# The first stage of a fused attention and SwiGLU kernel in another order

## The chip, the cores and the metric

The kernel runs on one core of one Trainium2 chip. The metric is the device time of one execution in microseconds (us). One execution was also recorded by the hardware profiler; times inside it are counted from the start of its span.

The engines are TensorE (PE, matrix products), VectorE (DVE), ScalarE (ACT), GpSimd (POOL) and SyncE (SP). Each works through its own instructions in order, and they meet by semaphores. Transfers (DMAs) are issued by SP, ACT and POOL; POOL's go through a queue of their own, the software queue.

## What is computed

Four batches, eight heads, 768 tokens, head size 64. Each token attends to the 96 tokens up to itself and to the first 8 of its batch (the global ones), with a bias that falls with the distance; then a feed-forward block over 3072 tokens.

```python
scores = scale * np.matmul(q, k.transpose(0, 1, 3, 2))
is_global = pos[None, :] < int(n_global)
is_local = (rel >= 0) & (rel < int(n_local))
keep = is_global | is_local
scores = np.where(keep, scores + bias, -1000000000.0)
a = softmax(scores)
x = (a @ v).transpose(0, 2, 1, 3).reshape(B * S, H * D)
g = x @ w_gate
out = g * sigmoid(g) * (x @ w_val) @ w_out
```

(512 columns to 1536 and back to 512.)

## The kernel before

**The order is written out.** A long string, ORDER, lists steps such as `T.1.0.0` or `x.0.1.0`. A table maps the name before the first point to a function, and the rest are its arguments. The steps are run one after the other under a manual schedule, so each engine does its instructions in the order in which the steps name them. An engine that waits holds up all that stands behind it on the same engine.

**Tiling.** Keys are cut in seven chunks of 120; to each chunk the 8 global keys are added, so that a chunk has 128 rows. A chunk's scores are for the 216 queries that can see it. Heads go in pairs (hp 0 to 3). Batch 0, the first to be worked on, is cut in two halves of 384 tokens, and each half's scores in two parts (u), one 432 wide per head (864 for the pair) and one 144 (288). A tile of the feed-forward block is half a batch (360 or 408 tokens).

**The steps of the first stage.**
- `fill` (L345): matmuls of constants, whose result is not used; each is 256 columns wide.
- `Lf` (L256) loads one head pair of the first half of keys or queries in float32 by SP or ACT; `cast` (L349) turns it into float16 on DVE or ACT. `Lh` (L260) loads other heads through POOL, where the transfer itself casts.
- `T` (L366): six transposes on PE, of one head pair and half of keys or queries. `k` (L379, L385) copies the transposed keys from PSUM into chunks on DVE or ACT and then spreads the eight global columns over all chunks on DVE. `q` (L395) copies the queries.
- `B` (L461): products of a slope times the identity (`sl`, L331) with the distances (L248, L253), which put the bias into the score bank. `c` (L474): the score products. `x` (L484): the exponential on ACT. `M` (L337) makes masks on ACT from the distances, and `m` (L502) multiplies by them; units with a bias need none.
- `w` (L537): denominator and numerators; `i` (L554, L555), `r` (L563), `p` (L574): the reciprocal of the denominator, its spread and the product that gives xT. `g`, `v` (L587): gate and value products, `t`, `s`, `h` (L594, L599, L609): the activation. `o` (L622): the output products; `e` (L632, L634): eviction on ACT and transfer on SP.
- `Lv` (L264) loads one chunk of the values, rows 8 and up. The rows 0 to 8 of chunks 1 to 6 hold the batch's first eight values. `LG` (L269) loads these for all four batches into a small tile vG; `G` (L277 by SP, L279 by an engine) copies them from there into the chunks. For chunk 0 the first rows are cleared.
- `D` (L432): transposes of later batches' keys and queries by DMA, issued on SP.

**PSUM.** Two double banks, S0 and S1, are taken in turn by scores and numerators; four single ones go to all others. So each second pair of score steps waits until the exponential of the one before last has been done.

**Around the change.** In ORDER, batch 0's first steps are: LG, the clearing and 16 fills; queries cast and transposed; keys cast on DVE, transposed and copied on DVE; then biases `B.1.1 B.1.0`, scores, and exponentials `x.0.1.0 x.0.1.1`, where the first unit sits in S1 and the second in S0; then the transposes of three more head pairs and `B.0.0`, which takes S0. Batch 0's global rows are copied by POOL in two halves (`G.0.1.4.P`, `G.0.4.7.P`), those of the others by SP (`G.1.0.7.S`, `G.2.0.7.S`, `G.3.0.7.S`). At the end, the last 128 tokens' output is made in two halves of 256 columns (`o.3.5.x.0` and `.1`), each with its eviction and transfer.

Of the kernel before, what the change touches and what calls it, by code (L numbers as in the profile page):

```python
# [10 lines left out]
FP16 = mybir.dt.float16  # L11
# [4 lines left out]
KC = 120  # L16
# [21 lines left out]
LG Li Z.0.P pre fill.14 sl.2 fill.2 Lf.A.1.0 cast.1.0.V sl.6 Ld.S T.0.0.1 q.0.0.V sl.3 Lf.A.1.1 dd  # L38
cast.1.1.A sl.1 T.1.0.1 Lf.S.0.1 cast.0.1.V Lh.0.0.4.8 T.1.0.0 k.1.0.V sl.0 Lf.S.0.0 cast.0.0.V
B.1.1 B.1.0 q.1.0.A c.0.1.0 M.5.0 c.0.1.1 M.1.1 T.0.0.0 k.0.0.V T.3.0.0 sl.4 k.3.0.V M.0.1 x.0.1.0  # L40
x.0.1.1 Lh.1.0.4.8 T.2.0.0 M.6.1 k.2.0.A M.7.1 B.0.0 c.0.0.0 x.0.0.0 B.0.1 c.0.0.1 x.0.0.1 T.2.0.1
T.3.0.1 q.3.0.V Lh.1.1.0.4 Lh.0.1.0.4 sl.5 T.1.1.0 Lh.1.1.4.8 q.2.0.V T.1.1.1 q.1.1.A Lv.0.1 k.1.1.V
T.0.1.1 c.0.3.1 Lv.0.2 Lv.0.0 B.2.0 Lh.0.1.4.8 Lw.0.0.0 x.0.3.1 c.0.2.0 q.0.1.V Lw.1.0.0 T.0.1.0
w.0.0.0.0 Lw.0.0.1 x.0.2.0 T.2.1.1 T.3.1.1 B.2.1 c.0.2.1 q.2.1.A sl.7 B.3.0 x.0.2.1 q.3.1.A
G.0.1.4.P c.0.3.0 x.0.3.0 Lw.1.0.1 M.3.0 w.0.0.0.1 i.0.0.0 Lw.0.1.0 m.0.3.1.P r.0.0.0 w.0.0.0.2
p.0.0.0.V T.3.1.0 T.2.1.0 w.0.1.0.0 i.0.1.0 B.1.2 c.0.1.2 r.0.1.0 w.0.1.0.1 k.3.1.A Lw.0.1.1
w.0.1.0.2 x.0.1.2 Lw.1.1.0 ga.0.0 Lw.1.1.1 ga.0.1 B.1.3 c.0.1.3 k.0.1.A p.0.1.0.V x.0.1.3 k.2.1.V
c.0.3.2 x.0.3.2 m.0.3.2.V g.0.3 gb.0.0 t.0.0 s.0.0 B.0.3 t.0.3 s.0.3 gb.0.1 t.0.1 Lw.0.2.1 c.0.0.2
c.0.0.3 x.0.0.3 s.0.1 v.0.3 h.0.3 v.0.0 x.0.0.2 v.0.1 Lw.0.2.0 h.0.1 g.0.4 g.0.7 L4.1.0 t.0.4 h.0.0
s.0.4 t.0.7 s.0.7 g.0.6 t.0.6 L4.0.0 M.4.1 s.0.6 ga.0.2 gb.0.2 t.0.2 M.3.1 v.0.4 Lv.0.5 h.0.4 v.0.6  # L50
c.0.2.3 s.0.2 m.0.0.2.P c.0.2.2 x.0.2.3 h.0.6 x.0.2.2 w.0.0.1.0 i.0.0.1 r.0.0.1 g.0.5 t.0.5
G.0.4.7.P s.0.5 v.0.2 v.0.7 M.2.1 h.0.7 g.0.8 h.0.2 g.0.9 M.5.1 t.0.8 s.0.8 v.0.5 Lv.0.3 M.6.0
g.0.11 Lv.0.4 t.0.9 s.0.9 h.0.5 Lv.0.6 Lw.1.2.0 t.0.11 s.0.11 g.0.10 t.0.10 c.0.3.3 s.0.10 m.0.2.3.V
m.0.2.2.P U.1.0 x.0.3.3 m.0.3.3.V U.0.1 U.1.1 kw.1.A U.0.0 qw.1.A w.0.0.1.1 w.0.0.1.2 p.0.0.1.V
w.0.1.1.1 w.0.1.1.0 Lw.1.2.1 Lr.1.0.6 w.0.1.1.2 i.0.1.1 c.1.1.1 Lr.1.0.7 v.0.9 r.0.1.1 p.0.1.1.V
kw.0.A Lr.1.1.7 qw.0.A v.0.8 x.1.1.1 h.0.8 h.0.9 M.7.0 v.0.10 Lr.1.0.4 g.1.6 Lr.1.1.4 c.1.0.0 t.1.6
x.1.0.0 c.1.0.1 D.1.3.0 v.0.11 h.0.11 h.0.10 g.1.0 t.1.0 s.1.0 x.1.0.1 c.1.1.0 g.1.9 t.1.9 g.1.7
s.1.6 t.1.7 s.1.9 g.1.1 s.1.7 x.1.1.0 g.1.3 v.1.0 t.1.3 Lr.1.0.5 h.1.0 v.1.6 D.1.2.0 c.1.0.2 s.1.3
h.1.6 c.1.1.2 K.1.3.A t.1.1 K.1.2.V g.1.5 s.1.1 x.1.1.2 M.2.0 M.0.0 v.1.9 h.1.9 v.1.7 t.1.5 h.1.7
Lr.1.1.6 Lr.1.1.5 D.1.3.1 s.1.5 g.1.2 t.1.2 x.1.0.2 s.1.2 D.1.2.1 v.1.5 g.1.11 t.1.11 h.1.5  # L60
m.1.0.1.P Lo.1 s.1.11 Lr.3.0.5 g.1.4 Lo.0 m.1.1.2.P v.1.3 h.1.3 t.1.4 m.1.0.2.V Lo.2 g.1.8 t.1.8
v.1.1 h.1.1 s.1.4 c.1.2.1 x.1.2.1 c.1.3.1 s.1.8 v.1.8 v.1.11 h.1.11 v.1.2 Lr.2.0.3 x.1.3.1 h.1.2
Lv.1.1 c.1.2.2 x.1.2.2 c.1.3.0 v.1.4 Lr.2.0.0 h.1.4 o.0.1.0 Z.1.V m.1.1.0.P M.4.0 Lr.2.0.2 m.1.3.1.V
G.1.0.7.S g.1.10 Lv.1.2 o.0.1.1 o.0.1.2 x.1.3.0 c.1.2.0 x.1.2.0 h.1.8 c.1.3.2 x.1.3.2 o.0.1.3 e.0.1
Lr.2.1.1 M.1.0 v.1.10 o.0.0.0 o.0.0.1 Lv.1.0 m.1.2.1.V m.1.1.1.V Lr.2.0.1 t.1.10 m.1.3.0.V o.0.0.2
o.0.0.3 o.0.2.0 o.0.2.1 m.1.2.2.V Z.2.V Lv.1.3 s.1.10 m.1.0.0.V w.1.0.1.0 e.0.0 w.1.0.0.1 w.1.0.0.0
h.1.10 m.1.2.0.P w.1.1.0.0 Lv.1.5 w.1.1.0.1 D.2.1.0 w.1.1.0.2 w.1.0.0.2 i.1.0.0 i.1.1.0 Lr.2.1.0
o.0.3.0 o.0.3.1 Lr.3.1.2 r.1.0.0 p.1.0.0.D D.2.0.0 o.0.3.2 o.0.3.3 Lv.1.6 r.1.1.0 Lv.1.4 Lr.2.1.4
p.1.1.0.D o.0.2.2 e.0.3 o.0.2.3 e.0.2 g.2.1 i.1.0.1 r.1.0.1 t.2.1 s.2.1 Lr.2.1.3 Lr.2.1.7 g.2.7
t.2.7 s.2.7 g.2.3 t.2.3 v.2.7 h.2.7 g.2.0 v.2.3 K.2.1.V Lr.3.0.1 g.2.5 s.2.3 K.2.0.V t.2.0 w.1.0.1.1  # L70
m.1.3.2.P w.1.1.1.1 w.1.1.1.0 D.2.0.1 s.2.0 w.1.1.1.2 Lr.2.1.2 D.2.1.1 i.1.1.1 w.1.0.1.2 o.0.4.0
t.2.5 s.2.5 Lr.2.0.7 Lr.2.0.6 o.0.4.1 o.0.4.2 o.0.4.3 p.1.0.1.D v.2.0 h.2.3 e.0.4 Lr.3.1.4 h.2.0
n.1.1.1 g.2.4 t.2.4 r.1.1.1 p.1.1.1.P D.2.3.0 v.2.1 h.2.1 s.2.4 g.2.11 t.2.11 s.2.11 g.2.2 t.2.2
# [27 lines left out]
G.3.0.7.S Lv.3.0 m.3.3.0.P v.5.10 h.5.0 g.5.1 t.5.1 o.2.1.0 h.5.10 w.3.1.0.0 s.5.1 i.3.1.0 w.3.1.0.1  # L101
# [15 lines left out]
o.3.5.3.0 o.3.5.0.1 o.3.5.1.1 o.3.4.1 o.3.4.2 e.3.5.0 o.3.4.3 e.3.4 o.3.5.2.1 o.3.5.3.1 e.3.5.1  # L117
"""
# [3 lines left out]
def kernel(  # L122
# [73 lines left out]
    vG = sb.tile([NG, B, H, D], FP16, name="vG")  # L196
# [47 lines left out]
    def ld_ident():  # L244
        nc.sync.dma_start(out=ident, in_=ident_dr.ap())
# [9 lines left out]
    def ld_first(e, i, hp):  # L255
        (nc.sync if e == "S" else nc.scalar).dma_start(  # L256
            out=h32[i][:, 2 * hp:2 * hp + 2, :], in_=tokens3(i, 0, 2 * hp, 2 * hp + 2))
# [10 lines left out]
    def ld_globals():  # L268
        nc.gpsimd.dma_start(  # L269
            out=vG.rearrange("p b h d -> p (b h) d"),  # L270
            in_=v[:, :, 0:NG, :].rearrange("b h p d -> p (b h) d"))

    def put_globals(b, c0, c1, e):
        src = vG[:, b, :, :].unsqueeze(1).broadcast_to([NG, c1 - c0, H, D])
        dst = v_of(b)[0:NG, c0:c1, :, :]
        if e == "S":
            nc.sync.dma_start(out=dst, in_=src)  # L277
        else:
            copy_on(e)(out=dst, in_=src)  # L279
# [68 lines left out]
    def cast(i, hp, e):  # L348
        copy_on(e)(out=h16[i][:, 0, 2 * hp:2 * hp + 2], in_=h32[i][:, 2 * hp:2 * hp + 2])  # L349
# [263 lines left out]
    def columns(side):  # L613
        return slice(0, DM) if side is None else slice(DM // 2 * side, DM // 2 * (side + 1))
# [73 lines left out]
```

## Time and profile before

| what | value |
|---|---|
| time, three runs | 241.26, 241.51, 241.61 us; median 241.51 |
| the profiled execution | 241.57 us |
| its span | 239.7 us (1.87 us lie around it) |
| busy PE, DVE, ACT, POOL | 97%, 66%, 49%, 53% of the span |
| mean clock granted to PE | 0.993 |
| DMA | 25.5 MB in 88,715 packets |

How to read it. A line of the timeline gives the start and the length of a run of like instructions in us, engine and line, operation, what is written and read, shape and number; in brackets stands how long the engine was idle before it and what ended the wait. Two instructions of one line may overlap on PE, which is pipelined, so their lengths don't add up. In a row of windows, the busy time of each engine in that stretch is followed by the granted clock of PE (1.00 is full) and by the DMA share, the mean busy share of the 16 DMA engines (it can exceed 1, since packets of several queues overlap).

### The profile page before, as it was taken

The numbers are of one execution on the slowest core, as the hardware profiler recorded it, in microseconds if no ns is written. First come the engines' busy times: TensorE is split into PE (matmuls) and PEld (weight loads), VectorE is DVE, ScalarE is ACT, GpSimd is POOL, SyncE is SP. The second block draws the span as 40 slices with busy tenths as digits, with TensorE's granted clock in tenths as the row PEclk, the third lists the DMA queues.
The fourth block names the chain that finished last, engine by engine and source line by source line (L and its number), as shares of the span: only waits on it lengthen the run. The fifth ranks groups of instructions, "written<-read, shape, count | busy, mean of one in ns | idle before, by whom it ended". The sixth has DMA issues, their size and how long they took to land.

```text
span 239.7 us, 5641 instructions
## 1 busy us (share of the span) xinstructions
PE 232.2 (97%) x2274; PEld 133.0 (55%) x2274; DVE 158.7 (66%) x351; ACT 117.8 (49%) x225; POOL 128.2 (53%) x136
## 2 busy tenths in 40 slices
PE   7799999999999999999999999999999999999994
PEld 4355666555455655555555555556566555565452
DVE  4587888687768785577876844687877843577000
ACT  3778777876505355666464446652142323232121
POOL 8996888599899098999974004699100000000000
PEclk9799999999999999999999999999999999999999
DMA  7999999999999999996999025323020110200042
GB/s 169 181 191 205 204 165 155 152 143 187 161 140 153 167 146 143 156 100 120 123 166 100 3 88 92 68 16 23 0 90 3 44 40 8 83 4 0 0 175 90
DMA packets 88715, 25.50 MB, mean 106 GB/s; under 512 B 78537, under 2 KB 85745, under 8 KB 88689
## 3 DMA queue, kind: packets, MB, share of 16 engines
q0 software_dynamic: 67520, 13.81, 68.8%
q1 hardware_dynamic: 20624, 10.94, 20.8%
q8 instruction: 18, 0.29, 0.5%
q10 hardware_dynamic: 544, 0.39, 0.5%
q14 instruction: 9, 0.07, 0.1%
HBM read 28.52 MB, written 6.29 MB: 145 GB/s over the span
## 4 chain that ended last, share of the span: by engine, by line
PE 93%; DVE 3%; ACT 2%; issue 0%; ACTq 0%
PE gps L587 27%; PE vps L587 26%; PE ops L622 25%; PE sc L474 5%; PE num L537 4%; PE den L537 2%; PE warm L345 1%; PE sc L461 1%; ACT at L484 1%; PE trs L366 1%; DVE qT L395 1%; DVE at L502 1%; PE trs L404 1%; DVE slopeI L331 1%; DVE xT L574 0%; ACT osb L632 0%
## 5 line engine op out<-in xcount | busy, mean ns | idle before, releaser
L587 PE MATMUL gps<-xT,wg 128*128 128x408 f16 (+1 forms) x384 | 72.9, 327 | 0.0
L594 ACT ACTIVATE th<-gps 128x360 f32<-128x360 f32 (+1 forms) x96 | 46.5, 491 | 53.0 <-PE gps L587 47.9
L587 PE MATMUL vps<-xT,wv 128*128 128x408 f16 (+1 forms) x384 | 72.5, 327 | 0.0
L609 DVE TENSOR_TENSOR hT<-vps,sl 128x360 f16<-128x360 f32 (+3 forms) x108 | 52.8, 509 | 23.6 <-PE vps L587 22.1
L599 DVE SCALAR_TENSOR_TENSOR sl<-th,gps 128x360 f32<-128x360 f32 (+1 forms) x96 | 51.6, 549 | 24.2 <-ACT th L594 22.9
L622 PE MATMUL ops<-wo,hT 128*128 128x512 f16 (+1 forms) x300 | 67.0, 371 | 0.0
L502 POOL TENSOR_TENSOR at<-at,masks 128x432 f16<-128x432 f16 (+3 forms) x36 | 47.8, 1345 | 29.1 <-ACT at L484 28.0
L587 PEld LDWEIGHTS <-wv 128*128 128x128 f16 x384 | 36.7, 98 | 26.8 <-issue 1.4
L587 PEld LDWEIGHTS <-wg 128*128 128x128 f16 x384 | 36.7, 98 | 25.6 <-issue 0.7
L484 ACT ACTIVATE at<-sc 128x864 f16<-128x864 f32 (+2 forms) x52 | 42.2, 840 | 12.7 <-PE sc L474 12.5
L622 PEld LDWEIGHTS <-hT 128*128 128x128 f16 x300 | 28.8, 98 | 30.0 <-issue 0.2
L632 ACT ACTIVATE osb<-ops 128x512 f32<-128x512 f32 (+1 forms) x25 | 14.3, 580 | 48.9 <-PE ops L622 47.1
L264 POOL DMA_DIRECT2D vS<-in_v_dram x28 | 25.5, 919 | 1.6 <-DVE vS L282 1.4
L305 POOL DMA_DIRECT2D qst<-in_q_dram x20 | 17.2, 875 | 0.0
L305 POOL DMA_DIRECT2D kst<-in_k_dram x20 | 17.2, 865 | 0.0
L474 PE MATMUL sc<-qT,kT 64*128 64x216 f16 (+4 forms) x232 | 15.0, 243 | 0.7 <-DVE slopeI L331 0.5
L574 DVE TENSOR_TENSOR xT<-num,rb 128x720 f16<-128x720 f32 (+1 forms) x15 | 14.1, 949 | 1.6 <-PE num L537 1.0
L474 PEld LDWEIGHTS <-kT 64*128 64x128 f16 x232 | 8.1, 94 | 10.6 <-issue 7.9
L554 DVE STREAM_TRANSPOSE dT<-den 128x384 f32<-128x384 f32 (+1 forms) x16 | 9.5, 595 | 4.3 <-PE den L537 4.0
L502 DVE TENSOR_TENSOR at<-at,masks 128x864 f16<-128x864 f16 (+2 forms) x21 | 10.5, 536 | 1.9 <-ACT at L484 1.9
L537 PE MATMUL num<-at,vS 128*32 128x216 f16 (+4 forms) x512 | 11.6, 233 | 0.0
L537 PEld LDWEIGHTS <-vS 128*32 128x32 f16 x512 | 9.1, 96 | 1.3 <-issue 1.1
(58 smaller groups left out, 114.5 us busy)
## 6 DMA issues: line engine op xcount, KB each, us to landing
out_dram<-osb SPq DMA_DIRECT2D x23, 256.0 KB, 2.1
vS<-in_v_dram POOLq DMA_DIRECT2D x24, 120.0 KB, 5.3
kst<-in_k_dram POOLq DMA_DIRECT2D x20, 96.0 KB, 5.1
qst<-in_q_dram POOLq DMA_DIRECT2D x20, 96.0 KB, 5.4
wg<-in_moe_w_gate_dram POOLq DMA_DIRECT2D x6, 256.0 KB, 8.4
wv<-in_moe_w_val_dram POOLq DMA_DIRECT2D x6, 256.0 KB, 8.0
wo<-in_moe_w_out_dram POOLq DMA_DIRECT2D x3, 512.0 KB, 8.1
k<-in_k_dram POOLq DMA_DIRECT2D x3, 192.0 KB, 6.4
```

The lines of the kernel that those rows point to most:

```text
L264: nc.gpsimd.dma_start(out=v_of(b)[NG:NG + n, c, :, :], in_=v[b, :, KC * c:KC * c + n, :].rearrange("h p d -> p h d"))
L305: nc.gpsimd.dma_start(out=rows_of(i, b, h // 2)[:, :, h % 2, :], in_=KQ[i][b, h].rearrange("(t p) d -> p t d", p=128))
L474: nc.tensor.matmul(sc[:, hi, col:col + n], lhsT=kTs[hp][r, 128 * c:128 * c + 128], rhs=qTs[b, hp][r, q0:q0 + n], start=fresh, stop=True, s ...
L484: nc.scalar.activation(out=at[:, :, 0:w], in_=scs.pop((b, hp, u))[:, :, 0:w], func=AF.Exp, scale=scale)
L502: ENG[e].tensor_mul(a2, a2, m[:, :, m0:m0 + n])
L537: nc.tensor.matmul(dst[r, o:o + n], lhsT=vSs[b][:, c, 4 * g + j, what - 1::2] if what else ones[:, 0:32], rhs=ats[b, hp, u][:, j % 2, col: ...
L587: nc.tensor.matmul(gv[t, f, which][:, 0:n], lhsT=w[:, c, 128 * f:128 * f + 128], rhs=xTs[t][:, c, 0:n], start=(c == 0), stop=(c == NC - 1))
L594: nc.scalar.activation(out=th[:, 0:n], in_=gv[t, f, 0][:, 0:n], func=AF.Tanh, scale=0.5)
L599: nc.vector.scalar_tensor_tensor(out=sl[:, 0:n], in0=gv[t, f, "t"][:, 0:n], scalar=1.0, in1=gv[t, f, 0][:, 0:n], op0=AluOp.add, op1=AluOp. ...
L609: nc.vector.tensor_mul(hT[:, f, at:at + c1 - c0], gv[t, f, 1][:, c0:c1], gv[t, f, "s"][:, c0:c1])
L622: nc.tensor.matmul(ops_t[key][:, 0:c.stop - c.start], lhsT=hT[:, f, r0:r0 + 128], rhs=wo[:, f, c], start=(f == 0), stop=(f == NFF - 1))
L632: nc.scalar.mul(out=osb[:, 0:n], in_=ops_t[key][:, 0:n], mul=0.5)
```

## The change

The first steps stand in another order.

- Of the 16 fills 10 stay at the start; four come after the first query transposes, one before the biases, four between key transposes and scores: 19 in all.
- The biases `B.1.1 B.1.0` (now in this order) are made ahead of the key transposes.
- Casts of the first keys are split, two heads, on DVE and ACT (`VA`); so are the copies of the first key pair: chunks 0 and 1 on DVE, chunk 2 and the part of chunk 3 on ACT.
- Scores and exponentials of the first pair: `c.0.1.1 x.0.1.1 c.0.1.0 x.0.1.0`.
- Masks M.1.1, M.5.0, M.6.1, M.7.1 are at other places.
- vG is gone. LG loads batch 0's global rows alone, straight into chunk 1, and stands behind the loads of values of batch 0's first chunks instead of ahead of everything. Chunk 2 gets them by a DVE copy (`G.0.2.3.V`), chunks 3 to 6 by one POOL copy (`G.0.3.7.P`). For batches 1 to 3, SP copies them from rows 8 to 16 of the batch's own chunk 0, so after that chunk has been loaded; in SP's order `G.1` now stands behind the output `e.0.1`, `G.2` behind `e.1.0`, and `G.3` after the load of batch 3's chunk 0.
- The last 128 tokens' second half is cut in two: columns 256 to 384 and 384 to 512, with 24 products of 128 columns in place of 12 of 256, and three evictions and transfers in place of two.

```diff
-LG Li Z.0.P pre fill.14 sl.2 fill.2 Lf.A.1.0 cast.1.0.V sl.6 Ld.S T.0.0.1 q.0.0.V sl.3 Lf.A.1.1 dd
-cast.1.1.A sl.1 T.1.0.1 Lf.S.0.1 cast.0.1.V Lh.0.0.4.8 T.1.0.0 k.1.0.V sl.0 Lf.S.0.0 cast.0.0.V
-B.1.1 B.1.0 q.1.0.A c.0.1.0 M.5.0 c.0.1.1 M.1.1 T.0.0.0 k.0.0.V T.3.0.0 sl.4 k.3.0.V M.0.1 x.0.1.0
-x.0.1.1 Lh.1.0.4.8 T.2.0.0 M.6.1 k.2.0.A M.7.1 B.0.0 c.0.0.0 x.0.0.0 B.0.1 c.0.0.1 x.0.0.1 T.2.0.1
...
+Li.S Z.0.P pre fill.10 sl.2 Lf.1.0.A cast.1.0.V sl.6 Ld.S T.0.0.1 q.0.0.V sl.3 fill.4 Lf.1.1.A dd
+cast.1.1.A sl.1 T.1.0.1 M.5.0 q.1.0.A fill.1 B.1.1 B.1.0 Lf.0.1.S cast.0.1.VA Lh.0.0.4.8 T.1.0.0
+k.1.0.VA Lf.0.0.S sl.0 cast.0.0.VA fill.4 c.0.1.1 x.0.1.1 c.0.1.0 x.0.1.0 T.0.0.0 k.0.0.V T.3.0.0
+sl.4 k.3.0.V Lh.1.0.4.8 T.2.0.0 M.0.1 k.2.0.A B.0.0 c.0.0.0 x.0.0.0 B.0.1 c.0.0.1 x.0.0.1 M.6.1
+M.7.1 T.2.0.1 T.3.0.1 q.2.0.V Lh.1.1.0.4 Lh.0.1.0.4 sl.5 T.1.1.0 Lh.1.1.4.8 q.3.0.V T.1.1.1 q.1.1.A
+Lv.0.1 k.1.1.V T.0.1.1 c.0.3.1 Lv.0.2 Lv.0.0 LG B.2.0 Lh.0.1.4.8 Lw.0.0.0 x.0.3.1 c.0.2.0 q.0.1.V
...
     def ld_globals():
         nc.gpsimd.dma_start(
-            out=vG.rearrange("p b h d -> p (b h) d"),
-            in_=v[:, :, 0:NG, :].rearrange("b h p d -> p (b h) d"))
+            out=v_of(0)[0:NG, 1, :, :], in_=v[0, :, 0:NG, :].rearrange("h p d -> p h d"))
 
     def put_globals(b, c0, c1, e):
-        src = vG[:, b, :, :].unsqueeze(1).broadcast_to([NG, c1 - c0, H, D])
-        dst = v_of(b)[0:NG, c0:c1, :, :]
+        vS = v_of(b)
+        src = vS[0:NG, 1, :, :] if b == 0 else vS[NG:2 * NG, 0, :, :]
+        src = src.unsqueeze(1).broadcast_to([NG, c1 - c0, H, D])
+        dst = vS[0:NG, c0:c1, :, :]
...
     def cast(i, hp, e):
-        copy_on(e)(out=h16[i][:, 0, 2 * hp:2 * hp + 2], in_=h32[i][:, 2 * hp:2 * hp + 2])
+        n = 2 // len(e)
+        for x, h in zip(e, range(2 * hp, 2 * hp + 2, n)):
+            copy_on(x)(out=h16[i][:, 0, h:h + n], in_=h32[i][:, h:h + n])
...
         if half == 0:
-            part(0, 3, 0, KC, 0)
-            part(3, 4, 0, cut * J2, 3 * pc)
+            if len(e) == 1:
+                part(0, 3, 0, KC, 0)
+            else:
+                part(0, 2, 0, KC, 0)
+                part(2, 3, 0, KC, 2 * pc, e[1])
+            part(3, 4, 0, cut * J2, 3 * pc, e[-1])
...
     def columns(side):
-        return slice(0, DM) if side is None else slice(DM // 2 * side, DM // 2 * (side + 1))
+        return slice(*((0, DM) if side is None else ((0, 256), (256, 384), (384, 512))[side]))
```

## The prediction

> **What bounds the kernel now.** I read the page first (busy shares, the clock row, the chain), then the table of busy time over the windows of the throttled clock, then TensorE, DVE and ACT in order of time over the first 20 us, then SP around 60 us and the last 5 us.
>
> ```profile
> PE 232.2 (97%) x2274; PEld 133.0 (55%) x2274; DVE 158.7 (66%) x351; ACT 117.8 (49%) x225; POOL 128.2 (53%) x136
> PEclk9799999999999999999999999999999999999999
> PE 93%; DVE 3%; ACT 2%; issue 0%; ACTq 0%
> ```
>
> TensorE (PE) is busy 232.2 of 239.7 us and is 93% of the chain that ended last. Its idle time is 1.19 us at the start, 2.3 us in four stalls before 13.4 us, two stalls of 0.3 and 0.4 us later, and 3.5 us of tail. So time is won where PE idles or runs at a low clock, which is before 20 us, and any new wait of PE later costs its whole length. The clock row has one low digit after the start.
>
> ```profile
> core 0: us, PE busy (x) PEld busy (x) DVE busy (x) ACT busy (x) POOL busy (x), PEclk, DMA share, GB/s
> 5.29:8.70 3.41, 1.68 (x28) 0.84 (x26) 2.62 (x11) 1.89 (x5) 3.41 (x5) 1.00 1.51 192
> 8.70:12.12 3.42, 3.18 (x36) 1.65 (x34) 1.67 (x8) 3.32 (x8) 3.11 (x5) 0.50 1.86 176
> 12.12:15.53 3.41, 2.99 (x65) 1.97 (x60) 3.08 (x8) 2.09 (x5) 3.32 (x5) 1.00 1.80 181
> ```
>
> The clock changes on a raster of 3.41 us: half until 5.29, full to 8.70, half to 12.12, full from there on. The window in which PE was busy 1.68 of 3.41 us (49%) is followed by half clock; the one with 2.99 us (88%) is not. The limit lies between.
>
> ```profile
> 6.76 0.36 PE L366 MATMUL trs<-ident,k 128*64 128x128 f16 x6 [1.26 <-DVE k L349]
> 7.05 0.66 PE L461 MATMUL sc<-dist,slopeI 128*128 128x144 f16 x4
> 8.18 0.42 PE L474 MATMUL sc<-qT,kT 64*128 64x216 f16 x6 [0.47 <-DVE slopeI L331]
> 8.54 1.05 PE L366 MATMUL trs<-ident,k 128*64 128x128 f16 x18
> 9.83 0.88 PE L461 MATMUL sc<-dist,slopeI 128*128 128x432 f16 x2 [0.24 <-ACT at L484]
> ```
>
> PE waits for the cast of the first keys, then for the copies behind their transposes (the slope named at 8.18 is only the last thing DVE had finished), then for a score bank that an exponential still holds.
>
> ```profile
> 6.36 0.34 DVE L349 CAST k<-k 128x384 f16<-128x384 f32 x1
> 7.16 0.62 DVE L379 COPY kT<-trs 128x360 f16<-128x360 f16 x2 [0.46 <-PE trs L366]
> 7.73 0.40 DVE L385 COPY kT<-kT 128x56 f16<-128x56 f16 x1
> ```
>
> ```profile
> 8.59 1.19 ACT L484 ACTIVATE at<-sc 128x864 f16<-128x864 f32 x2 [1.19 <-PE sc L474]
> ```
>
> The keys had landed at 6.11, but DVE was at other work and cast them only from 6.36. Of ACT's two exponentials the 864-wide one runs first (8.59 to 9.47) and the 288-wide one ends at 9.78. The 288-wide one holds bank S0, which the next biases need, so PE starts those at 9.83.
>
> **The head, step by step.** *Keys.* The cast is split over DVE and ACT and DVE has nothing else to do: start 6.14, and half of ACT's 0.51 (the row of its 384-wide cast) with some fixed cost is 0.30, so 6.45. Transposes 6.50 to 6.86 (0.36). The split copy doesn't run side by side: in the order of instructions ACT's part waits for DVE's. DVE 240-wide 0.40, ACT 120-wide some 0.27 (between its 0.20 for 24 and 0.37 for 240) and 24-wide 0.20: 0.87 us, so about 7.75, where before the last copy ended at 8.13. The copy of the global columns (0.40) is now DVE's beside ACT. *Biases* cost PE 0.66 us beside the cast instead of behind the transposes. *Exponentials.* Scores near 7.8, the 288-wide exponential (0.41) done at about 8.3 instead of 9.78. Then S0 is free before PE has done the 18 transposes of the next three head pairs. They take 0.058 us a pair at full clock and 0.10 at half, so 8.1 to 8.7, and the biases of the next unit start at 8.7 to 9.0 instead of 9.83.
>
> *Fills.* 19 instead of 16, three groups of them in PE's waits. With the transposes of the second queries (0.36), one fill (0.2), biases (0.66), key transposes (0.36), four fills (0.45), scores (0.42) and the first of the next transposes, PE is busy 2.4 to 2.8 us of the window from 5.29 to 8.70, 70 to 82%. That lies between 49% and 88%, nearer the upper end: I take it that the clock stays full.
>
> *What that is worth.* With both, I carried every dependence of the order through to 25 us with the durations of the rows of before. The same walk puts before's first gate product at 19.19 (trace 19.36) and v.0.3 at 23.13 (23.15). It gives 0.95 us (0.9 to 1.05) less at the gate products near 25 us; with half clock in one window more, 0.0 to 0.2. Next in line are the global rows: they now come after the values of chunk 0, and DVE copies them ahead of the first dT at 15.78. Values of chunk 0 landed at 14.85; 192 packets of 128 bytes at 31 ns over 16 engines are gone ahead of them (0.37), so the 64 left land at about 14.6, and dT starts at 14.8 to 15.0. If they land 1 us later, the gain is gone, since PE has nothing else to do there. The POOL copy at 12.14 (1.45 us) goes; DVE's slope at 12.92 no longer ends only with it (0.73 instead of 0.19): 0.5 us on DVE, within the walk. Unknown: the keys' landing at 6.11, since the loads that now compete have packets of 51 ns instead of 31: 0.3 us either way.
>
> **The rule that speaks against it.** The page "TensorE: Matmul & The Clock Gate", section "HAM oscillation — how this bites in real kernels", gives the rule as no PE idle gap above about 3.4 us, in which case these fills would buy nothing: only the 0.1 us of the half-clock walk would remain, and the time would be near 241.4. The window of 5.29 to 8.70 had no idle gap longer than 1.26 us and was followed by half clock, so I go by the busy share of the window.
>
> **Later, where the gain is spent.** *At 36 us.* The second values landed at 35.99 and 36.23 and the product that reads them came with 0.37 us to spare. The queue is full from the start, so transfers come only 0.37 us earlier, while PE comes 0.95 earlier: 0.95 − 0.37 − 0.37 = 0.2 us lost there. The longer POOL copy (8x2048 instead of 8x1536, +0.45 us) lies under that backlog (7 us from issue to landing) and costs nothing; if the queue ran dry behind it, 0.45.
>
> *Batches 1 to 3.* The rows no longer come from the small tile loaded at the start, but from rows that the batch's own chunk 0 brings. SP therefore waits for that load.
>
> ```profile
> 60.14 0.89 SPq L277 DMA_DIRECT2D vS<-vG  x1
> 64.37 3.00 SPq L634 DMA_DIRECT2D out_dram<-osb  x2
> ```
>
> ```profile
> 67.59 0.51 PE L537 MATMUL den<-at,ones 128*32 128x104 f16 x20
> 67.93 0.41 PE L537 MATMUL num<-at,vS 128*32 128x216 f16 x12
> ```
>
> Chunk 0 of batch 1 landed at 65.10, issued at 59.31. With everything 0.5 us earlier SP's copy is issued from about 64.6, behind the out of e.0.1 (whose issue ends at 64.73 now, 64.2 then). From issue to landing this copy took 3.4 us for batch 2 and 3.1 for batch 3, and 5.5 for batch 1, where the DMA share of the windows from 60 to 63 us was 2.4; from 66 to 67 us it is 0.37. So it lands at 67.7 to 68.0, and PE wants it at 67.93 − 0.6 = 67.3: I take a stall of 0.35 (0 to 0.7). Behind the waiting issue stand the next out and the key transpose at 67.54, wanted by nobody until 75.28. For batch 2, chunk 0 landed at 105.65, the copy goes behind the out at 108.84 and lands near 112.3 against 112.83: nothing, but the transposes behind it start 0.73 later with 0.65 to spare, so up to 0.1. Batch 3: 150.60 + 3.1 is far ahead of 166.9.
>
> *Moved masks* (M.1.1, M.5.0, M.6.1, M.7.1): 0.4 to 0.56 us each on ACT, 49% busy; M.5.0 fills ACT's wait at 4.9 to 5.5 and delays the second query copy by up to 0.4, before keys are there: nothing. *Tail.*
>
> ```profile
> 235.64 1.04 ACT L632 ACTIVATE osb<-ops 128x512 f32<-128x512 f32 x2 [2.21 <-PE ops L622]
> ```
>
> The last 256-wide eviction began at 236.29, when ACT was free, and took 0.38. Three thirds instead of halves leave 128 columns: some 0.28, and one eviction and one issue (0.35) more before it. PE's twelve extra matmuls cost nothing in columns. I take −0.1, from +0.2 to −0.2.
>
> **Sum.** Profiled execution 241.57 (span 239.7 and 1.87 around it): −0.95 + 0.2 + 0.35 − 0.1 = −0.5, 241.07. The median of the runs, 241.51, lies 0.06 lower: **241.0**. A measurement of this kernel tells a change from none from about 0.2%, 0.48 us.
>
> **Rivals.**
> - *A, the sum above* (0.38): 240.7 to 241.4.
> - *B, the copies land in time* (0.24): SP's copy lands by 67.3, and the gain is kept: −0.75 to −1.2, about 240.5. For it: the thin queue at 66 us. Against it: it needs a landing in 2.7 us, and the least seen is 3.1.
> - *C, the head gains nothing* (0.20): one window drops to half clock after all, or the split copies, which don't run side by side, or a later landing of keys or global rows, eat the start. −0.1 in the head, nothing at 36 us, +0.15 at 67 us, −0.1 in the tail: about 241.45 (241.1 to 241.8). For it: the limit is only known to lie between 49 and 88%, and the window after it must hold too.
> - *D, a new wait at 67 us, slower* (0.18): the copy of batch 1's rows takes 5.0 to 5.5 us as it did under load, lands at 69.6 to 70.1, and PE, with no other work in its order, stands 2.3 to 2.8 us: −0.85 + 2.0 to 2.8, about 242.9 (242.4 to 243.4). It decides as soon as issue to landing is over 4 us. For it: three loads that land between 65.1 and 66.3 and two more issued before 67.7. Against it: the share of 0.37 at 66 us.
>
> Faster by over 0.2% (below 241.03): 0.17 of A, all of B and 0.01 of C, 0.42. Within 0.2%: 0.21 of A, 0.14 of C, 0.35. Slower: 0.05 of C, 0.18 of D, 0.23. The range leaves out the upper part of D and a little of B: 240.2 to 242.4.
>
> **What would show it.** Right: no half-clock window after 5.3 us; biases of the second unit before 9.1; first gate product at 18.3 to 18.6; a stall of 0.2 at 35 to 36 us, and one of 0.3 before a numerator near 67.4 that names SP's copy. Wrong: the clock row low at 9 or 13 us, DVE waiting for the global rows beyond 15.2, no stall at 67 us (B), or one above 1 us (D).

## The result, and the profile after

The changed kernel takes 248.18 us (median of 247.42, 247.86, 248.49 and 252.84), the kernel before 241.39 us; the ratio is 1.0265, with a 95% interval of 1.0238 to 1.0292: some 6.4 us slower. Forecast were 241.0 us and a range to 242.4. The execution of 252.84 us counts as a slow one and is left out of the ratio, but it is the one that was profiled, so this trace serves to find the places, and sizes are taken from the experiments.

The page of the changed kernel: busy time, the clock, the chain.

```profile
PE 235.1 (94%) x2289; PEld 133.5 (53%) x2289; DVE 157.7 (63%) x351; ACT 118.7 (47%) x230; POOL 127.6 (51%) x135
PEclk9999999999997999999999999999999999999998
PE 72%; DMA 12%; POOL 6%; issue 4%; DVE 3%; ACT 2%; POOLq 0%; SPq 0%; ACTq 0%; DVEq 0%
```

PE is busy only 2.9 us more, but the chain now runs through DMA (12%) and POOL (6%), which were not in it before. The low clock digit has moved from the second slice (6 to 12 us) to the thirteenth (75 to 82 us). What PE waited for (total us, times, longest):

```profile
PE num L544 <- issue: 4.0, 1, 4.0
PE vps L594 <- DMA wv<-in_moe_w_val_dram: 1.6, 1, 1.6
PE warm L346 <- DVE ones L324: 1.2, 1, 1.2
PE gps L594 <- DVE xT L581: 0.8, 1, 0.8
PE num L544 <- DMA vS<-vS: 0.6, 2, 0.3
```

Only the third was there before. To see what each one costs, I paired the n-th denominator, numerator, gate and value products of the two traces and subtracted their starts (us, against the profiled execution of before; the column heads are the places in before):

| kernel | den 14.8 | gate 21.0 | num 36.4 | value 42.0 | gate 73.4 | num 112.8 | gate 120.2 | value 172.9 | span |
|---|---|---|---|---|---|---|---|---|---|
| changed | -0.54 | +0.55 | +0.95 | +2.61 | +8.40 | +8.73 | +9.65 | +10.14 | +11.4 |

The loss comes in steps, each with a place. The head, which should have won 0.95, loses 0.55 by 21 us and 0.4 more by 30; 1.7 come at 41 us; 5.8 at 71 us; 0.3 and 0.9 at 113 and 120; 0.5 before 173; and 1.2 after the last value product, in the tail. Without the 5.8 at 71 us that makes 5.6 us. The other three executions lose some 6.4, which leaves about 0.8 us for that place in them: an estimate, as none of them was traced. Their mean clocks are 0.996 to 0.999; a window of half clock costs 1.7 of some 245 us, 0.007, so they hold none behind a stall.

*The head.* Timeline of PE, then of DVE, in the changed kernel:

```profile
7.25 0.36 PE L369 MATMUL trs<-ident,k 128*64 128x128 f16 x6
8.41 0.42 PE L481 MATMUL sc<-qT,kT 64*128 64x144 f16 x6 [0.27 <-DVE slopeI L332]
9.41 0.78 PE L369 MATMUL trs<-ident,k 128*64 128x128 f16 x18 [0.57 <-DVE k L352]
10.12 0.54 PE L468 MATMUL sc<-dist,slopeI 128*128 128x432 f16 x2
12.36 0.36 PE L369 MATMUL trs<-ident,k 128*64 128x128 f16 x6 [0.46 <-DMA k<-in_k_dram]
```

```profile
6.71 0.49 DVE L352 CAST k<-k 128x192 f16<-128x192 f32 x1 [1.17 <-DMA k<-in_k_dram]
9.09 0.26 DVE L352 CAST k<-k 128x192 f16<-128x192 f32 x1 [0.73 <-DMA k<-in_k_dram]
16.11 0.40 DVE L280 COPY vS<-vS 8x512 f16<-8x512 f16 x1 [2.04 <-DMA vS<-in_v_dram]
```

The keys that were there at 6.11 and 6.96 land at 6.68 and 9.07, and the late global rows hold DVE until 16.1, with the first reciprocal behind them.

*41 us.* POOL in the kernel before, then in the changed one:

```profile
24.88 1.53 POOL L502 TENSOR_TENSOR at<-at,masks 128x208 f16<-128x208 f16 x2 [1.13 <-ACT at L484]
27.78 2.54 POOL L264 DMA_DIRECT2D vS<-in_v_dram  x3
```

```profile
23.77 0.94 POOL L264 DMA_DIRECT2D vS<-in_v_dram  x1 [0.33 <-PE sc L481]
28.58 1.53 POOL L509 TENSOR_TENSOR at<-at,masks 128x208 f16<-128x208 f16 x2 [3.87 <-ACT masks L338]
30.07 1.88 POOL L280 COPY vS<-vS 8x2048 f16<-8x2048 f16 x1
31.91 2.53 POOL L264 DMA_DIRECT2D vS<-in_v_dram  x3
```

POOL stands 3.87 us for a mask that ACT makes late, and the loads behind it go out 4.1 us later than before (31.91 instead of 27.78), the last value weights among them.

*71 us.* SP and PE in the changed kernel:

```profile
68.83 0.90 SPq L278 DMA_DIRECT2D vS<-vS  x1
69.84 0.35 SPq L641 DMA_DIRECT2D out_dram<-osb  x1
70.36 4.60 SPq L439 DMA_TRANSPOSE kN<-kst  x2
```

```profile
70.20 0.51 PE L544 MATMUL den<-at,ones 128*32 128x104 f16 x20
74.71 0.42 PE L544 MATMUL num<-at,vS 128*32 128x216 f16 x12 [4.00 <-issue]
```

SP could issue the copy of batch 1's rows only once chunk 0 had landed (68.78); before it went out at 60.14. The last of the copy lands at 74.62 by its semaphore, and the numerators begin at 74.71, 5.9 us behind the issue: the wait that the profile calls "issue" is for this copy. The window of 3.41 us in which PE stood is followed by one of half clock (busy time of PE, PEld, DVE, ACT, POOL, then the granted clock):

```profile
71.96:75.37 3.41, 0.66 (x36) 0.69 (x40) 0.00 (x0) 0.00 (x0) 3.41 (x5) 1.00 1.74 117
75.37:78.78 3.41, 3.41 (x62) 2.08 (x49) 3.04 (x7) 0.00 (x0) 3.41 (x4) 0.50 1.92 126
```

*The tail.* ACT in the changed kernel:

```profile
245.46 0.60 ACT L639 ACTIVATE osb<-ops 128x512 f32<-128x512 f32 x1 [0.25 <-PE ops L629]
247.07 0.28 ACT L639 ACTIVATE osb<-ops 128x128 f32<-128x128 f32 x1 [1.01 <-DMA out_dram<-osb]
248.20 0.28 ACT L639 ACTIVATE osb<-ops 128x128 f32<-128x128 f32 x1 [0.85 <-DMA out_dram<-osb]
```

The last two evictions wait for an earlier output to land: the output tiles are two in turn, and a third eviction needs the first one's tile back.

### The profile page after: what moved, and what is told of

It is laid out like the page before. It is cut to its first block, busy times and chain, and to the rows that moved or that the text cites. A ratio compares the mean times of both kernels' runs of the same rounds, so it can differ in the third digit from the quotient of the medians.

```text
span 251.1 us, 5683 instructions
## 1 busy us (share of the span) xinstructions
PE 235.1 (94%) x2289; PEld 133.5 (53%) x2289; DVE 157.7 (63%) x351; ACT 118.7 (47%) x230; POOL 127.6 (51%) x135
## 4 chain that ended last, share of the span: by engine, by line
PE 72%; DMA 12%; POOL 6%; issue 4%; DVE 3%; ACT 2%; POOLq 0%; SPq 0%; ACTq 0%; DVEq 0%
PE ops L629 23%; PE gps L594 21%; PE vps L594 20%; POOL at L509 4%; PE sc L481 3%; DMA q<-in_q_dram 3%; PE num L544 3%; DMA k<-in_k_dram 3%; DMA kN<-kst 2%; DMA wv<-in_moe_w_val_dram 2%; PE den L544 2%; DVE xT L581 1%; DMA vS<-vS 1%; ACT at L491 1%; POOL vS L264 1%
## 5 line engine op out<-in xcount | busy, mean ns | idle before, releaser
L629 PE MATMUL ops<-wo,hT 128*128 128x512 f16 (+2 forms) x312 | 67.8, 366 | 0.0
L639 ACT ACTIVATE osb<-ops 128x512 f32<-128x512 f32 (+2 forms) x26 | 14.5, 564 | 55.3 <-PE ops L629 48.6
L544 PE MATMUL num<-at,vS 128*32 128x216 f16 (+4 forms) x512 | 12.6, 241 | 4.9 <-issue 4.0
L481 PE MATMUL sc<-qT,kT 64*128 64x216 f16 (+4 forms) x232 | 14.7, 240 | 0.8 <-DVE xT L581 0.5
L544 PEld LDWEIGHTS <-vS 128*32 128x32 f16 x512 | 9.8, 99 | 6.8 <-issue 6.3
(60 smaller groups left out, 112.8 us busy)
```

The costliest lines, as they stand in the source:

```text
L481: nc.tensor.matmul(sc[:, hi, col:col + n], lhsT=kTs[hp][r, 128 * c:128 * c + 128], rhs=qTs[b, hp][r, q0:q0 + n], start=fresh, stop=True, s ...
L544: nc.tensor.matmul(dst[r, o:o + n], lhsT=vSs[b][:, c, 4 * g + j, what - 1::2] if what else ones[:, 0:32], rhs=ats[b, hp, u][:, j % 2, col: ...
L629: nc.tensor.matmul(ops_t[key][:, 0:c.stop - c.start], lhsT=hT[:, f, r0:r0 + 128], rhs=wo[:, f, c], start=(f == 0), stop=(f == NFF - 1))
```

## The experiments

My theory after this trace: three parts of the change each add a wait of their own (rows from the own chunk, the late mask M.1.1, the third eviction), and the head loses to the loads that took the small packets' place. The rival: the queue as a whole is late because of the new start, and the later stalls only follow from that. Times are medians, with the kernel before on the same chip beside them, and the ratio with its interval.

**M.1.1 back** (the changed kernel with one step moved).

```diff
-L4.0.0 M.1.1 M.4.1
+L4.0.0 M.4.1
-T.1.0.1 M.5.0 q.1.0.A
+T.1.0.1 M.5.0 M.1.1 q.1.0.A
```

> Only M.1.1 goes back to the start: it is made on ACT straight after M.5.0, in ACT's wait of 5.3 to 6.0 us, instead of at 28 us. Theory: in the changed kernel POOL's mask product at 28.6 waited 3.9 us for this mask, the copy of the global rows and four loads behind it on POOL were issued 4 us later, and PE stood 1.56 us at 41.6 us for the last value weights. So the stall at 41.6 goes and the time falls by about 1.6 us from 247.9: 246.3 (246.0 to 246.6). Rival, the queue is late by itself (its first loads land 1.2 us later than before): the weights land as late as now, and less than 0.4 us is won.

Measured 247.45 beside 242.16 (1.0191, 1.0123 to 1.0259): the fall is not clear of the spread in time, and the traced execution is the longest of the four (249.38 us). What the trace does show is that the stall at 41 us is gone and POOL's mask product begins at 24.83:

```profile
24.83 1.53 POOL L509 TENSOR_TENSOR at<-at,masks 128x208 f16<-128x208 f16 x2 [1.05 <-ACT at L491]
26.31 1.88 POOL L280 COPY vS<-vS 8x2048 f16<-8x2048 f16 x1
28.15 2.53 POOL L264 DMA_DIRECT2D vS<-in_v_dram  x3
```

The paired differences are -0.01 at 42 us (changed kernel: +2.61), then +4.68 at 73 us, as PE stood 3.1 us there.

**Rows of batches 1 to 3 from the small tile again** (changed kernel; the tile is loaded late).

```diff
-        src = vS[0:NG, 1, :, :] if b == 0 else vS[NG:2 * NG, 0, :, :]
+        src = vS[0:NG, 1, :, :] if b == 0 else vG[:, b, :, :]
...
-Lv.1.0 G.1.0.7.S
+m.1.3.1.V G.1.0.7.S
...
```

> Only the global rows of batches 1 to 3 go back to the small tile, which is now loaded behind the last value weights (192 packets, near 38 us), and SP's copies stand where they stood before. Theory: PE's stall ahead of batch 1's numerators (4.0 us in the profiled execution, with a window of half clock behind it; less in the quicker ones) and the two of 0.3 us at 121 and 177 us come from SP's wait for chunk 0's load. They go, and the time is 244.4 (243.6 to 245). Rival, the values themselves land late because the whole queue is late: the stall of PE stays at 70 us and names a load of values, 247 to 248.

246.24 beside 242.16 (1.0133, 1.0065 to 1.0200). The waits at the numerators of batches 1 to 3 and the one at 120 us are gone: the paired difference stays at +3.33 from 42 us to the end of the value products. What is left is the late mask (+3.6 between 36 and 42 us: a stall of 1.93 and a window of half clock behind it) and the tail. The direction is as expected, the size is not: with before 0.8 us higher on this chip, the time is still 1.0 us above the 244.4 that I expected and some 0.4 above the upper end.

**The small packets first again** (changed kernel; all global rows loaded at the start into a tile that nobody reads).

```diff
-Li.S Z.0.P
+LA Li.S Z.0.P
```

> Only one thing is added: the 256 small packets of all batches' global rows are loaded at the very start again, ahead of all other loads of POOL, into a tile that nobody reads. Theory: in the changed kernel POOL's first big load shares the DMA engines with the first two key loads, which land 0.6 and 2.1 us later than before (6.7 and 9.1 us instead of 6.1 and 7.0), and the head loses what its order wins. With the small packets in front the keys land at 6.1 and 7.0 again, the second biases start before 9.1, the first gate product comes near 18.5 instead of 20, and the time falls by 1.2 to 1.6 us to 246.5. Rival, the start is late for another reason (the biases ahead of the key transposes at half clock, the split copies that run one after the other): the keys land earlier and the gate product hardly moves, 247.5 to 248.2 with the 0.4 us of more packets.

249.91 beside 242.16 (1.0331, 1.0287 to 1.0375): no gain, rather a loss. Half of the theory held: the keys land at 6.18 and 7.12, and the first denominators come 1.43 us earlier than before. But DVE still waits for the late rows (to 15.5), at 21 us only 0.11 is left, and with the late mask PE stands 2.32 us at 41 us, with half clock behind it. My claim that the head's loss lasts to the end fell here.

**All three put back**: the three edits above in one kernel, with the tile that is loaded first as the source of the rows. New head and split tail remain.

> The three together: M.1.1 back, all global rows of batches 1 to 3 from the small tile, and that tile loaded first. What is left of the change is the order of the head and the split tail. Theory: without its three new waits the head's order is worth what was forecast for it, 0.7 to 1.0 us against the kernel before: 240.6 (240.3 to 240.9). Rival, the head's order wins nothing by itself (clock, split copies in series): 241.2 to 241.8; and if it loses, above 242.

242.82 beside 242.16 (1.0045, 1.0011 to 1.0078). The three waits are the bulk of the loss, but the head's 0.7 to 1.0 us don't show: the paired differences are -1.41 at 14.8 us, -0.44 at 21 us, -0.27 from 42 us on, and +1.1 in the span. So the head keeps 0.27 and the tail loses 1.3.

**Batch 0's rows from the small tile too** (the kernel above, without the late load).

```diff
-        src = vS[0:NG, 1, :, :] if b == 0 else vG[:, b, :, :]
+        src = vG[:, b, :, :]
...
-Lv.0.0 LG B.2.0
+Lv.0.0 B.2.0
-q.3.1.A G.0.2.3.V
+q.3.1.A G.0.1.3.V
```

> As the run with all three put back, but batch 0's global rows also come from the small tile: DVE copies them to chunks 1 and 2, and the late load of them is gone. Theory: with the order of the head the first denominators come 1.4 us earlier than before, but DVE then waits 1.9 us (13.2 to 15.2) for the late load, and only 0.4 us is left at the first gate product of 21 us. Without that wait the gate and value products from 21 us on come 0.9 to 1.4 us earlier than before (part of it lost again at 36 to 40 us to loads that come no earlier), and the time is 0.4 to 0.9 us below the run with three put back. Rival: DVE waits for PE or for POOL there in any case, and it is the same within 0.2 us.

242.70 beside 242.19 (1.0022, 0.9978 to 1.0067): the same, against my theory. The mechanism was right, its worth wrong. DVE's wait of 1.94 us at 15.17 is gone, and the gate products of 21 us come 1.36 earlier than before instead of 0.44. But then PE runs into late loads: at 20.45 us it waits 0.30 for gate weights (0.47 of the gain is gone by 21.3), and at 36 us for the second values:

```profile
36.09 1.02 PE L550 MATMUL num<-at,vS 128*32 128x216 f16 x52 [0.29 <-DMA vS<-in_v_dram]
```

From 42 us on it is 0.31 ahead, as with the wait. The last second values land at 36.21 here, at 36.23 in before and at 36.09 in the kernel above: what the head wins ahead of that ends there, but for 0.3 us.

**The split tail alone** (before with it), **and with a tile of its own for the last 128 columns**.

```diff
-        osb = sb2.tile([128, DM], FP32, name="osb", tag="osb")
+        last = side == 2
+        osb = sb2.tile([128, n if last else DM], FP32, name="osb",
+                       tag="osl" if last else "osb", bufs=1 if last else 2)
```

> The kernel before with the split tail alone. Theory: the output tiles are two in turn, so the third eviction of the last rows waits until the transfer of the one before last has landed (in the changed kernel it began 2.0 us after the last product, just as that transfer landed): the time is 1.2 to 1.4 us above before. Rival, as forecast: 0.1 us below before.

> The same split tail, but the last 128 columns have an output tile of their own. Theory: the last eviction begins when its products are done, about 236.0 of the span, and the end comes 0.1 to 0.4 us earlier than before: the forecast's term, once its wait is taken away. Rival: the third transfer by itself costs the time (its issue, and its landing behind two others), and it stays over 0.5 us above before.

243.12 and 241.35 beside 242.19 (1.0032, 1.0000 to 1.0065; 0.9980, 0.9946 to 1.0015). ACT in the first and in the second:

```profile
235.06 0.77 ACT L633 ACTIVATE osb<-ops 128x512 f32<-128x512 f32 x2 [1.89 <-PE ops L623]
237.85 0.28 ACT L633 ACTIVATE osb<-ops 128x128 f32<-128x128 f32 x1 [2.03 <-DMA out_dram<-osb]
```

```profile
235.01 0.77 ACT L635 ACTIVATE osb<-ops 128x512 f32<-128x512 f32 x2 [1.89 <-PE ops L623]
235.97 0.28 ACT L635 ACTIVATE osb<-ops 128x128 f32<-128x128 f32 x1 [0.19 <-PE ops L623]
```

The wait for the tile is the cost: from the last value product to the end of the span, the split tail takes 1.3 us more than before in the first, 0.2 less in the second. In time the first is 0.3% slower with an interval that begins at none, so the size rests on the trace.

**Rows from the own chunk alone** (before with the source and the places of the changed kernel).

```diff
-        src = vG[:, b, :, :].unsqueeze(1).broadcast_to([NG, c1 - c0, H, D])
+        src = (vS[NG:2 * NG, 0, :, :] if b else vG[:, b, :, :]).unsqueeze(1).broadcast_to([NG, c1 - c0, H, D])
...
-G.1.0.7.S g.1.10
+g.1.10
...
+Lv.1.0 G.1.0.7.S
...
```

> The kernel before with one thing of the change alone: SP copies the global rows of batches 1 to 3 from the batch's own chunk 0, at the changed kernel's places. Everything else, the head too, is as before. Theory: PE stands 2 to 4 us ahead of batch 1's numerators near 68 us, with a window of half clock behind it where the stall is over 3 us, some 1.3 us more for batch 2 (0.3 at the numerators, 0.8 behind the delayed transposes) and 0.3 to 0.5 for batch 3: 245.5 (244 to 248), and it varies more from run to run than before. Rival, the wait is only so long because the changed head makes all loads later: under 1 us, 242.3.

244.53 beside 242.19 (1.0096, 1.0061 to 1.0131): 2.3 us, near the lower end of what I expected. In its trace PE waits for batch 1 only 0.35 us: SP issues at 64.49, and the numerators start 3.5 us later.

```profile
68.03 0.42 PE L538 MATMUL num<-at,vS 128*32 128x216 f16 x12 [0.35 <-issue]
```

Batch 2 costs more: 0.36 at the numerators and 0.96 at the gate of 120 us. SP's copy stands ahead of the key transpose, which is issued 0.9 us later (111.53 instead of 110.65) and lands 3.0 us later (117.86 instead of 114.83); ACT waits 1.8 us for it, with the tanh and an eviction behind. Batch 3 costs 0.66. The single ten executions lie between 243.56 and 249.07.

**The late mask alone** (before with M.1.1 at the late place).

```diff
-c.0.1.1 M.1.1 T.0.0.0
+c.0.1.1 T.0.0.0
...
-L4.0.0 M.4.1
+L4.0.0 M.1.1 M.4.1
```

> The kernel before with M.1.1 alone at the changed kernel's late place (made near 27.5 us instead of 7 us). Theory: POOL's mask product, which began at 24.9, waits for it until some 27.9, the four loads and the two blocks of value weights behind it on POOL are issued 3 us later, and PE stands 1.5 to 2.5 us near 41 us, with a window of half clock behind it where its share falls low enough: 1.5 to 3 us above before. Rival, forecast's: POOL's loads are far ahead of their use (7 us from issue to landing), nothing.

243.51 beside 241.70 (1.0083, 1.0050 to 1.0117): 2 us. POOL and PE:

```profile
27.81 1.53 POOL L502 TENSOR_TENSOR at<-at,masks 128x208 f16<-128x208 f16 x2 [4.60 <-ACT masks L337]
30.71 2.53 POOL L264 DMA_DIRECT2D vS<-in_v_dram  x3
35.44 0.75 POOL L312 DMA_DIRECT2D wv<-in_moe_w_val_dram  x1
```

```profile
38.78 0.48 PE L587 MATMUL vps<-xT,wv 128*128 128x360 f16 x2
40.90 2.78 PE L587 MATMUL vps<-xT,wv 128*128 128x360 f16 x10 [1.64 <-DMA wv<-in_moe_w_val_dram]
```

The stall is 1.64 us, but ten value products take 2.78 us there, as the window behind the stall has half clock: 3.4 us in all in this execution, the slowest of its five. The mean clocks of the five are 1.000 (242.36 and 243.51), 0.990, 0.993 and 0.992, so not every execution pays for a window. In the other three it can also be one of the head's, as in before.

**New head with none of the three, all rows from the tile; its twin with the old head; and the change mended.** The first is the kernel with all rows from the tile, its last 128 columns in their own output tile. The twin is the kernel before with that tail. The mended kernel keeps the change's idea (no small tile; batch 0's 64 packets first), but loads chunk 0 of batches 1 and 3 where chunks 1 and 3 were loaded, and lets SP copy ahead of the outputs; M.1.1 is early and the last 128 columns have their own tile.

```diff
-h.1.2 Lv.1.1 c.1.2.2
+h.1.2 Lv.1.0 c.1.2.2
...
-m.1.3.1.V g.1.10
+m.1.3.1.V G.1.0.7.S g.1.10
...
-o.1.0.3 e.1.0 Lv.2.0 G.2.0.7.S
+Lv.2.0 G.2.0.7.S o.1.0.3 e.1.0
...
```

> The changed kernel's head with all global rows from the small tile loaded first, M.1.1 early, and the split tail with an output tile of its own: all of the change without the waits found. Theory: the head's gain ends at 36.2 us, where the last second values land in every kernel so far, so this is no faster than the kernel before with that tail alone (its twin in this call): equal within 0.3 us, some 0.3 to 0.5 below before. Rival: the head's gain of some 0.4 us at the first gate products is kept in part, 0.3 to 0.6 below the twin.

> The same kernel as the one with the last 128 columns in their own output tile, as twin for the run beside it: 0.2 to 0.5 us below before.

> The change as it is meant, without the small tile, but with its waits put where they end early: batch 0's rows (64 packets) loaded first, M.1.1 early, chunk 0 of batches 1 and 3 loaded in the place of chunk 1 and chunk 3, SP's copies ahead of the outs where they stood before, the last 128 columns in their own output tile. Theory: no stall ahead of the numerators of batches 1 to 3, the queue up to 36 us 0.4 us shorter, so that here the head's gain shows for that much: 0.4 to 0.9 us below before, 0.2 to 0.5 below the twin. Rival: chunk 0 of batch 1 still lands late under load, or the transposes behind SP's copies do: 0.3 to 2 us above before.

241.68, 241.33 and 241.47 beside 241.70; ratios 0.9996 (0.9972 to 1.0019), 0.9995 (0.9971 to 1.0019), 0.9995 (0.9975 to 1.0016): none can be told from before or from each other. The first is no faster than its twin, as the theory had it; the gain of 0.2 to 0.5 that I expected of the tail, and that of 0.4 to 0.9 of the mended kernel, are not confirmed. In the first one's trace the head wins nothing at all (-0.04 from 14.8 us on): the clock became full only at 9.91 us. In the mended kernel's, with full clock from 9.73, it wins 0.39. In the mended kernel SP's copy goes out at 61.98 and PE has no stall left after 13.2 us but the one of 0.3 that before has at 105. It is 0.31 ahead from 42 us on, and an eviction in its tail waited 1.0 us for an output that landed late.

**The three parts together on the old head, and the new head without them.** The first joins the edits of own rows, late mask and split tail on the kernel before; the second is the changed kernel with M.1.1 back, the rows from the late-loaded tile and the last 128 columns in their own output tile.

> The old head, with its load of all global rows first, and the three costly parts together: rows of batches 1 to 3 from the own chunk 0, M.1.1 late, split tail with two output tiles in turn. Theory: the parts make each other longer (a PE that comes later at 41 us meets a POOL whose loads are late too, and the copy of batch 1's rows then runs among more loads), and the sum is that of the whole change: 246.5 to 248.5, against 241.5 before. Rival, they only add up and the rest is the new head's: 246.2 to 246.8 and the run beside it 1 to 1.5 us above before.

> The new head with its late load of batch 0's rows and without the three: rows of batches 1 to 3 from the small tile loaded near 38 us, M.1.1 early, the last 128 columns in their own output tile. Theory: the head is hidden by the loads that land at 36.2 us, so the time is that of before within 0.4 us: 241.2 to 241.9. Rival: the late first keys and the late rows cost 1 to 1.5 us that last: 242.5 to 243.

248.35 and 242.47 beside 242.07 (1.0292, 1.0265 to 1.0318; 1.0036, 1.0006 to 1.0067). The three parts alone make the whole loss (2.9%, against 2.65% for the whole change), on a head and a queue that start as before. The new head without them is 0.4% slower (0.06 to 0.67%), some 0.9 us: more than the 0.4 us of the theory, near its rival. Its traced execution was its longest (249.19 us), so the place of this rest stays open. The rival of the start of this section is answered: the new start isn't needed for the later stalls. The paired differences of five kernels:

| kernel | den 14.8 | gate 21.0 | num 36.4 | value 42.0 | gate 73.4 | num 112.8 | gate 120.2 | value 172.9 | span |
|---|---|---|---|---|---|---|---|---|---|
| own rows alone | -1.09 | -1.09 | -1.09 | -0.43 | +0.11 | +0.47 | +1.43 | +2.09 | +2.1 |
| three parts | -0.32 | -0.32 | +0.07 | +3.54 | +4.08 | +4.43 | +5.56 | +6.07 | +7.5 |
| new head, all rows from the tile, split tail | -1.36 | -1.36 | -0.88 | -0.31 | -0.31 | -0.31 | -0.31 | -0.31 | +1.2 |
| the same, tail with own tile | -0.04 | -0.04 | -0.04 | -0.04 | -0.04 | +0.24 | +0.24 | +0.24 | +0.6 |
| old head, tail with own tile | -0.80 | -0.80 | -0.80 | -0.30 | -0.30 | -0.31 | -0.31 | -0.31 | -0.5 |

The ratios of the parts alone add up to 2.1% (0.96, 0.83, 0.32), together they give 2.9%. The parts' intervals are some 0.3% to either side, so a part of the gap can be noise. In the traces the parts don't make each other longer, against my theory: in the run with all three, the mask costs 3.5 us (alone 3.4, each with a half-clock window), batch 1 0.54 (0.54), batch 2 1.5 (1.3), batch 3 0.5 (0.7) and the tail 1.5 (1.3). All five executions of the three parts have a mean clock of 0.986 to 0.991, so each pays for half clock; of the late mask alone at most three of five do. That this is the whole of the gap is argued, not shown.

## Why the prediction was wrong, step by step

In the traced execution of the changed kernel the misses are: the masks (forecast nothing, 1.7 us), batches 2 and 3 (up to 0.1, 1.7), the tail (-0.1, 1.2) and the head with the place at 36 us (-0.75, +0.95); batch 1 (0.35) was passed by some half a microsecond in the other executions, by the estimate above.

- **"Moved masks ... nothing."** This step failed. I weighed only ACT's free time and not who waits for the mask: POOL's product, and behind it in POOL's order the loads of the second values and of the last value weights. Its cost alone is 2 us, a stall of 1.6 at 41 us and often a slow window behind it.
- **Batch 1's rows.** The mechanism was named, as the stall of 0.35 in the sum and as rival D. With the old head the stall measured 0.35 us, in the kernel with this part alone and in the one with all three; with the changed head it was 0.9, 3.1 and 4.0. Issue to numerators was 3.5 us in the first two and 3.9, 5.0 and 5.9 in the others. But 3.1 and 4.0 come from the executions of 249.38 and 252.84 us, the longest of their kernels, so the 0.35 of the sum was about right for most executions (0.35 to some 0.8), and D came true only in long ones. That the changed head makes the copy slower isn't shown. D's own terms, by the way, give 242.65 to 243.45, not 242.4 to 243.4.
- **Batch 2, "up to 0.1".** Mis-sized: 0.36 at the numerators and about 1.0 behind the transposes. A transpose issued 0.9 us later landed 3.0 us later, and ACT, in order, held a tanh behind it.
- **Batch 3, "150.60 + 3.1".** I read the wrong load: 150.60 is another chunk's. Chunk 0 was issued at 160.45 and landed at 163.96, and the copy takes 3.0 more, so the numerators at 166.9 had no slack: 0.5 to 0.7 us.
- **Tail, "-0.1".** Wrong in sign: +1.2 to +1.3. I counted the eviction and the issue, but not that two output tiles serve three evictions. With a tile of its own the same split takes 0.2 us less in one trace and 0.04 less in its twin's, and its time can't be told from before.
- **Head, "-0.95".** Three terms were wrong. The keys' landing ("0.3 us either way") moved by up to 0.57 us for the first load and by 1.0 to 2.1 for the second, in the four traces without small packets in front. The global rows landed at 14.7 to 16.1 us in six traces, not at 14.6. And the yardstick was one execution: its half-clock window of 8.7 to 12.1 us is missing in four of six other traces with the old head, two of which (full from 9.8 and from 3.9 us) bring the first denominators 0.8 and 1.1 us earlier without any change to the head.
- **What the order is worth** therefore depends on the clock. With the new head and full clock from 5.7 to 7.4 us, the first denominators come 1.4 us earlier than in the profiled execution of before (three traces, keys there at 5.7 to 6.2), which is 0.3 more than the old head with full clock from 3.9. With full clock only from 9.91 they come 0.04 earlier, though the keys were there at 5.57, and the old head with full clock from 9.78 comes 0.76 ahead of that. Most of that (0.69) is there at the first key transpose, in these lines of the new head and then of the old: at half clock, fills and biases keep PE busy up to 7.45 us, and the keys, cast by 7.00, wait for it; with the old order PE is idle before them and takes them at 6.76.

```profile
4.74 1.03 PE L352 MATMUL warm<-ones 128*128 128x256 f16 x4
6.35 1.17 PE L474 MATMUL sc<-dist,slopeI 128*128 128x144 f16 x4
7.45 0.53 PE L375 MATMUL trs<-ident,k 128*64 128x128 f16 x6
```

```profile
6.76 0.53 PE L367 MATMUL trs<-ident,k 128*64 128x128 f16 x6 [1.19 <-DVE k L350]
7.22 1.14 PE L462 MATMUL sc<-dist,slopeI 128*128 128x144 f16 x4
```

- **"0.2 us lost" at 36 us.** The place was named, its size was not: this was the real limit. The second values land at 36.1 to 36.4 us in ten of sixteen traces, with either head, and of gains of 0.8 to 1.4 us at 14.8 only 0.2 to 0.4 is left at 42 us where no late mask comes between. So the head is worth about nothing in the time, in the orders that were run.
- **Fills and clock.** Right as far as it goes: once the clock had become full (at 7.1 us in the changed kernel), none of nine traces with the new head has a window of half clock before 30 us; of seven with the old head three have. But the sum took full clock from 5.29 us for granted, the place of one execution's windows, and in four of the nine it comes at 9.4 to 9.9.

## What to carry over

For each step that is moved, list who waits for its result and what stands behind that waiter on its queue: here a mask of 0.5 us on an engine with half its time free cost 2 us, by way of POOL's loads. Where a copy's source is changed, its new issue time is the landing of that source, and a tile that rotates over two buffers makes a third use wait for the first one's transfer. Before a gain at the start is counted, look for the next place where PE meets a load that doesn't move: it is spent there. And compare two starts only in executions whose clock becomes full at a like time.

## What the runs showed of the hardware

- The raster of the clock's windows lies differently in each execution (first full window from 3.9 to 10.6 us), so one kernel's head is timed with and without a half-clock window. (Before the first full window the clock is read from the length of the matmuls, a fill takes 0.42 us at half clock and 0.27 at full.) From full clock, the ten windows up to 230 us in which PE was busy 19 to 49.5% were followed by half clock, and those with 49.9% and more stayed full. It is no clean rule: among the last output products three windows with 42, 45 and 47% stayed full. From half clock, twelve windows with 65 to 86% stayed at half, one with 79% and all with 87% and more went to full. The Trainium skill, "TensorE: Matmul & The Clock Gate", section "HAM oscillation — how this bites in real kernels", names idle gaps above some 3.4 us as the limit; here a window whose longest gap was 1.26 us (busy 49%) and one with a stall of 1.64 (busy 48%) were followed by half clock, so the busy share tells more than the longest gap.
- SP's copy of the global rows, the same bytes each time, took from 3.1 us (batch 3) to 5.9 us (batch 1) from issue to the start of the numerators that wait for it.
- In eleven traces with 256 packets of 128 bytes at the head of POOL's queue, the first two key loads by SP landed at 5.6 to 6.2 and 6.5 to 7.1 us; in four with POOL's big loads in front, at 6.1 to 6.7 and 8.0 to 9.1; with only 64 such packets in front (the mended kernel, one trace), at 7.0 and 8.2.
